# Eight row buffers, scatters by tile and later weight splits at the seam between attention and experts

## The chip, the cores and the metric

The kernel runs on one core of one Trainium2 chip. A time is the device time of one execution in microseconds (us). Besides that, one execution was profiled; its trace counts from the start of its own span. PE is the matrix engine (TensorE), DVE the vector engine, ACT the scalar engine, POOL is GpSimd, and SP issues most of the transfers.

## What is computed

Three stages follow each other. The output of attention, 1536 tokens of 512 numbers, is routed to two of eight experts for each token, and what comes back runs through a dense layer.

```python
# attention: 2 batches x 8 heads x 768 tokens, head size 64
k_sum = k.reshape(B, H, nb, 32, D).max(axis=3); v_sum = v.reshape(B, H, nb, 32, D).mean(axis=3)
scores_l = where(|i - j| < 16, scale * q @ k.T, -1e9)        # a window
scores_s = scale * q @ k_sum.T + log(32)                     # and 24 block summaries
a = softmax(concat(scores_l, scores_s)); attn = a @ concat(v, v_sum)
# routed experts: x is attn as 1536 x 512
noisy = x @ w_gate + log1p(exp(x @ w_noise)) * noise
top2, weights = two best of noisy, softmax over the two
out[n] = sum over its two experts e of weight * (relu(x[n] @ w1[e]) @ w2[e])     # 512 -> 1024 -> 512
# dense layer
h = out @ w_in; r = relu(h); y = (r * r) @ w_out                                  # 512 -> 2048 -> 512
```

## The kernel before

**Attention, with its own planner.** The attention stage is a list of nodes (`class Plan`), each with an engine, a cost, nodes that it depends on and buffers that it takes from a pool. The planner plays the list through in a model of the engines and emits the instructions in the order in which its model starts them, those with the longest chain of costs behind them first. So costs and edges decide the order, and each engine then runs its instructions in that order.

**Token rows.** The 1536 tokens are twelve tiles g = 0 to 11 of 128 rows. PE turns the attention output of a tile into rows in PSUM (L437), and DVE scales them into a buffer `xrow` (L441), one of six (pool `xr`). The gate works in four groups (`GROUPS`: tiles 0 to 5, 6 to 8, 9, and 10 with 11); it gives each row two places (k = 0 and 1) in the DRAM buffer `xg`, which is ordered by expert.

**Scatters.** POOL sends each tile's rows twice to `xg` with an indirect DMA (L461), 24 in all. Ahead of each goes a memset of a one-row tile `spacer` of 640 columns (L460), 1 column for tiles 6 to 8. A buffer of `xrow` is free when both scatters of its tile have landed. The order is tile 0 twice, then k = 0 of tiles 1 to 5, and then k = 1 of tiles 1 to 5, since the k = 0 nodes are chained and have the longer chain behind them.

**Expert 0's rows.** When the scatters of tiles 0 to 8 have landed, SP reads expert 0's part of `xg` back (`rows_load`, L522). The scatters of tiles 9 to 11 come after that. Those three tiles go to expert 0 on a shorter way too: DVE makes a one-hot matrix `pick` of each tile (L593), PE multiplies it into PSUM (`pull`, L510, from hi and lo parts `xpick` of the rows), and adds the rows read back (`rows_add`, L529). ACT (L249) and DVE (L254) split the sum into `xh` and `xl`.

**Weights.** Matrix products are done in three passes of fp32r, so each weight tile `wr` of 128x1024 is split into `wh` (ACT, L206) and `wl` (DVE, L210). The splits 0 and 1 belong to attention's planner and have a pool of their own; split 2 is the first that uses the pool `wsp1`, which is opened when attention's pools are closed and takes their memory.

**Units.** From there the order is written out in one loop: 64 units of the experts (8 for each), then 48 of the dense layer. Unit g does `h_unit` (12 matmuls of w1 with relu, hh on ACT L834, hl on DVE L835) and then `y_unit` of unit g - 1 (12 matmuls of w2, which need hh and hl). In the same loop stand the weight splits, and steps of other work at given units: `tables()` (routing tables on DVE, L929 to L1005, with a scatter of 24 zero rows to `xg`, L982), `fill(e)` (an indirect DMA of POOL that writes zero rows behind the rows of expert e, L920), `x_load(e)` (SP reads expert e's rows, L234), then DVE's transposes (L240).

**Blending.** Towards the end of the experts a token tile's two expert rows are gathered and blended (`mix`, L1210, stored to DRAM by L1215), read back with 32x32 blocks exchanged (`swap`, four transfers, L1219), and transposed by DVE (`flip`, L1230). The five numbers of `G0` say at which unit after its start each of these steps of a tile in 0 to 3 stands (gather, mix, swap, flip, and the split behind it). `y_store` (L858 to L866) writes an expert's output with eight transfers.

Of the kernel before, what the change touches and what calls it, by code (L numbers as in the profile page):

```python
# [19 lines left out]
QT = S // 128  # L20
# [3 lines left out]
E = 8  # L24
# [34 lines left out]
SPACE = 640  # L59
# [14 lines left out]
G0 = (0, 4, 5, 8, 9)  # L74
# [3 lines left out]
class Plan:  # L78
# [6 lines left out]
    def node(self, eng, cost, fn, *deps, take=(), wait=0.0, after=()):  # L85
        n = {"id": len(self.nodes), "eng": eng, "cost": cost, "fn": fn, "deps": deps, "after": after, "take": take,
             "wait": wait, "free": {}}
        self.nodes.append(n)
        return n
# [18 lines left out]
    def run(self):  # L108
        after = {n["id"]: [] for n in self.nodes}
        need = {}  # L110
        for n in self.nodes:
            before = {d["id"] for d in (*n["deps"], *n["after"])}
            need[n["id"]] = len(before)
            for d in before:
                after[d].append(n)
        then = {i: list(a) for i, a in after.items()}
# [33 lines left out]
def moe_pipeline_kernel(ctx: ExitStack, tc: tile.TileContext, qT, kT, vW, mk, idm, wg, noise, w1, w2, out):  # L150
# [105 lines left out]
    def attention(ctx):  # L256
# [4 lines left out]
        xr_p = ctx.enter_context(tc.tile_pool(name="xr", bufs=6))  # L261
# [17 lines left out]
        zt = ac.tile([128, CAP], F32, name="zt")  # L279
        ioc = ac.tile([128, CAP], F32, name="ioc")  # L280
        spacer = ac.tile([1, SPACE], F32, name="spacer")
# [4 lines left out]
        for b in range(B):  # L286
# [4 lines left out]
                     "gw": 1, "xr": 6, "k": LBUF, "w": LBUF, "q": LBUF},  # L291
# [167 lines left out]
        def scatter(g, k):  # L459
            nc.gpsimd.memset(spacer[:, 0:1] if 6 <= g < DIRECT else spacer, 0.0)  # L460
            i = nc.gpsimd.indirect_dma_start(out=xg, out_offset=bass.IndirectOffsetOnAxis(ap=slot_i[:, g, k:k + 1], axis=0),  # L461
                                             in_=xrow[g], in_offset=None)
            for j in scat:
                tc.declare_no_dep(i.ins, j.ins, reason="every slot is a row of its own")
            scat.append(i)
# [190 lines left out]
        for u in range(len(heads)):  # L656
# [38 lines left out]
            if u == 1:  # L695
                wvals_n = load(0.9, lambda: (nc.sync.dma_start(out=wg_sb, in_=wg), nc.sync.dma_start(out=nz, in_=noise)),
                               after=[last])
                zero_n = load(2.4, lambda: nc.sync.dma_start(
                    out=xg[0:CAP, :].rearrange("r d -> (r d)").rearrange("(p a c) -> p a c", p=128, a=4),
                    in_=zt[:, None, :].to_broadcast([128, 4, CAP])), set_n, after=[wvals_n])  # L700
# [41 lines left out]
        for g0, n in GROUPS:  # L742
# [11 lines left out]
            p_t["L", g0] = rt.tile([128, QT, 16], F32, name="L", bufs=len(GROUPS))[:, 0:n, :]  # L754
# [23 lines left out]
            for g in range(g0, g0 + n):  # L778
                for k in range(2):
                    sct[g, k] = node("G", 1.28 if 6 <= g < DIRECT else 1.77, lambda g=g, k=k: scatter(g, k), slot_n, xr_n[g], zero_n, *late,  # L780
                                     after=() if k or g >= DIRECT else list(sct.values())[-1:], wait=1.0)
# [12 lines left out]
        for i in range(W0):  # L794
            split = [node("A", 1.04, lambda i=i: w_hi(i), wl[i], after=[*split, slots_n[6]])]
            node("V", 1.22, lambda i=i: w_lo(i), *split)
# [121 lines left out]

    def fill(e):
        nc.gpsimd.indirect_dma_start(  # L920
            out=xg.rearrange("(g r) d -> g (r d)", r=4),
            out_offset=bass.IndirectOffsetOnAxis(ap=gi[0:XC // 4, e:e + 1], axis=0),
            in_=z4[0:XC // 4], in_offset=None)

    def tables():
# [45 lines left out]
        def by_expert(out, a):  # L971
# [4 lines left out]
        ri, gf = tbp.tile([128, 1], I32, name="tb_ri"), t("gf", E)  # L976
        tt(ri[0:n3], p[0:n3, 1, 0:1], rc[0:n3], OP.add)
        ts(gf, p[:, 0, 0:E], p4, OP.is_gt, NTOK / 4, OP.mult)
# [3 lines left out]
        nc.gpsimd.indirect_dma_start(out=xg, out_offset=bass.IndirectOffsetOnAxis(ap=ri[0:n3, 0:1], axis=0),  # L982
                                     in_=z4[0:n3, 0:DM], in_offset=None)
# [440 lines left out]
```

## Time and profile before

| what | value |
|---|---|
| runs | 678.84 us median of 3 (675.65, 678.84, 681.6) |
| the profiled execution | 677.83 us, of which its span is 675.8 us |
| mean granted clock of PE in it | 0.979 of full speed |
| PE busy | 637.6 us (94%) |
| DVE busy | 442.7 us (66%) |
| ACT busy | 366.2 us (54%) |
| POOL busy | 118.8 us (18%) |

In 40 slices of 16.9 us the page shows PE's busy tenths and its granted clock (tenths of full speed, 5 is 1.2 GHz and 9 about 2.4 GHz):

```profile
PE   5878776998999999999999999999999999999995
PEclk9989976999999999999999999999999999999998
```

The first seven slices, to 118 us, are attention and the seam to the experts. From the eighth on PE is busy nearly without a break. A time in what follows is a start in the trace; "[3.25 <-X]" behind an instruction is the idle time of its engine ahead of it and what ended it.

### The profile page before, as it was taken

What the parts mean: (1) busy time and instruction counts of PE and PEld (TensorE: products, weight loads), DVE (VectorE), ACT (ScalarE), POOL (GpSimd) and SP (SyncE); (2) the same over time, 40 slices, a digit from 0 to 9 for tenths busy, and PEclk for the clock granted to TensorE, in tenths of its full rate; (3) what the DMA queues carried; (4) which work ended last, traced back from release to release, by engine and by line L of the source; (5) the groups of instructions that cost most, each with busy time, mean ns of one, the idle gap of its engine ahead of it and who ended that gap; (6) DMA issues with size and microseconds to landing.
All of it is one profiled execution on the core that took longest, in us unless ns stands there. A gap on an engine that the chain in (4) does not pass through costs nothing. (4 is left out here: it accounts for less than half of the span.)

```text
span 675.8 us, 11334 instructions
## 1 busy us (share of the span) xinstructions
PE 637.6 (94%) x4062; PEld 572.0 (85%) x4062; DVE 442.7 (66%) x984; ACT 366.2 (54%) x708; POOL 118.8 (18%) x178
## 2 busy tenths in 40 slices
PE   5878776998999999999999999999999999999995
PEld 4766675898999999999999998888888888888884
DVE  4777856559687878677678867666555566544442
ACT  3846561456575667476667666654444454433431
POOL 4013385411001001700023001300043000300002
PEclk9989976999999999999999999999999999999998
DMA  8985135579999988788879888765356643333201
GB/s 215 233 206 180 49 157 214 196 218 327 367 280 326 290 293 252 237 234 273 265 245 389 249 280 244 271 157 161 119 160 196 186 144 110 141 108 96 92 1 66
DMA packets 72308, 138.96 MB, mean 206 GB/s; under 512 B 8873, under 2 KB 40313, under 8 KB 71462
## 3 DMA queue, kind: packets, MB, share of 16 engines
q1 hardware_dynamic: 66134, 115.92, 56.7%
q0 software_dynamic: 6112, 22.25, 8.7%
q8 instruction: 34, 0.56, 0.3%
q14 instruction: 28, 0.23, 0.1%
HBM read 103.27 MB, written 34.88 MB: 204 GB/s over the span
## 5 line engine op out<-in xcount | busy, mean ns | idle before, releaser
L813 PE MATMUL ph<-xl,wh 128*128 128x512 f32 (+8 forms) x448 | 162.4, 363 | 0.3 <-DVE xl L254 0.3
L811 PE MATMUL ph<-xh,wh 128*128 128x512 f32 (+8 forms) x448 | 162.7, 363 | 0.0
L812 PE MATMUL ph<-xh,wl 128*128 128x512 f32 (+8 forms) x448 | 162.3, 362 | 0.0
L210 DVE TENSOR_TENSOR wl<-wr,wh 128x1024 fp32r<-128x1024 f32 x112 | 136.7, 1221 | 37.9 <-ACT wh L206 35.3
L206 ACT ACTIVATE wh<-wr 128x1024 fp32r<-128x1024 f32 x112 | 117.5, 1049 | 13.1 <-DMA wr<-in_w_dram 8.0
L813 PEld LDWEIGHTS ph<-xl,wh 128*128 128x128 f32 x448 | 84.2, 188 | 8.3 <-DVE xl L254 0.7
L811 PEld LDWEIGHTS ph<-xh,wh 128*128 128x128 f32 x448 | 84.3, 188 | 7.6
L812 PEld LDWEIGHTS ph<-xh,wl 128*128 128x128 f32 x448 | 84.3, 188 | 7.6
L813 PE MATMUL acc<-hl,wh 128*128 128x416 f32 (+7 forms) x256 | 87.8, 343 | 1.6 <-DVE hl L835 1.6
L811 PE MATMUL acc<-hh,wh 128*128 128x416 f32 (+7 forms) x256 | 87.7, 343 | 0.8 <-ACT hh L834 0.8
L812 PE MATMUL acc<-hh,wl 128*128 128x416 f32 (+7 forms) x256 | 87.6, 342 | 0.0
L828 ACT ACTIVATE hr<-ph 128x512 f32<-128x512 f32 x48 | 28.7, 598 | 98.1 <-PE ph L813 95.8
L829 DVE SCALAR_TENSOR_TENSOR hg<-ph,hr 128x512 f32<-128x512 f32 x48 | 33.2, 692 | 66.9 <-ACT hr L828 64.4
L834 ACT ACTIVATE hh<-ph 128x416 fp32r<-128x416 f32 (+7 forms) x64 | 32.2, 503 | 80.5 <-PE ph L813 75.4
L812 PE MATMUL acc<-wh,hl 128*128 128x512 f32 x192 | 74.8, 390 | 0.0
L813 PE MATMUL acc<-wl,hh 128*128 128x512 f32 x192 | 74.7, 389 | 0.0
L811 PE MATMUL acc<-wh,hh 128*128 128x512 f32 x192 | 74.7, 389 | 0.0
L835 DVE SCALAR_TENSOR_TENSOR hl<-ph,hh 128x416 fp32r<-128x416 f32 (+7 forms) x64 | 36.5, 570 | 32.9 <-ACT hh L834 31.5
L832 DVE TENSOR_TENSOR hl<-hg,hh 128x512 fp32r<-128x512 f32 x48 | 33.3, 693 | 33.5 <-ACT hh L831 33.5
L831 ACT ACTIVATE hh<-hg 128x512 fp32r<-128x512 f32 x48 | 30.3, 632 | 38.0 <-DVE hg L829 37.2
L813 PEld LDWEIGHTS acc<-hl,wh 128*128 128x128 f32 x256 | 48.2, 188 | 2.3 <-DVE hl L835 2.2
L811 PEld LDWEIGHTS acc<-hh,wh 128*128 128x128 f32 x256 | 48.2, 188 | 1.2 <-ACT hh L834 1.1
(255 smaller groups left out, 921.4 us busy)
## 6 DMA issues: line engine op xcount, KB each, us to landing
wr<-in_w_dram SPq DMA_DIRECT2D x64, 512.0 KB
wr<-w2f SPq DMA_DIRECT2D x48, 512.0 KB
cr<-in_w_dram SPq DMA_DIRECT2D x32, 512.0 KB
w2f<-c SPq DMA_DIRECT2D x32, 256.0 KB
vB<-in_vW_dram SPq DMA_DIRECT2D x8, 576.0 KB
xin<-xg SPq DMA_DIRECT2D x16, 208.0 KB
kB<-in_kT_dram SPq DMA_DIRECT2D x16, 200.0 KB
yg<-ys SPq DMA_DIRECT2D x16, 192.0 KB
```

The lines of the kernel that those rows point to most:

```text
L206: nc.scalar.activation(out=hi_t[i], in_=raw_t[i], func=AF.Copy)
L210: nc.vector.tensor_tensor(out=lo_t[i], in0=raw_t.pop(i), in1=hi_t[i].bitcast(F32), op=OP.subtract)
L811: nc.tensor.matmul(out=o, lhsT=wh, rhs=xh, start=first, stop=False)
L812: nc.tensor.matmul(out=o, lhsT=wl, rhs=xh, start=False, stop=False)
L813: nc.tensor.matmul(out=o, lhsT=wh, rhs=xl, start=False, stop=last)
L828: nc.scalar.activation(out=r[:, 0:n], in_=p[:, 0:n], func=AF.Relu)
L829: nc.vector.scalar_tensor_tensor(out=gg[:, 0:n], in0=p[:, 0:n], scalar=0.0, in1=r[:, 0:n], op0=OP.max, op1=OP.mult)
L831: nc.scalar.activation(out=hh[:, 0:n], in_=gg[:, 0:n], func=AF.Copy)
L832: nc.vector.tensor_tensor(out=hl[:, 0:n], in0=gg[:, 0:n], in1=hh[:, 0:n].bitcast(F32), op=OP.subtract)
L834: nc.scalar.activation(out=hh[:, 0:n], in_=p[:, 0:n], func=AF.Relu)
L835: nc.vector.scalar_tensor_tensor(out=hl[:, 0:n], in0=p[:, 0:n], scalar=0.0, in1=hh[:, 0:n].bitcast(F32), op0=OP.max, op1=OP.subtract)
```

## The change

It has five parts.

1. `xr` has eight buffers in place of six. Room comes from the tile `L` of the gate, which now has as many columns as its group needs, and from `spacer`, which is gone: the memset ahead of a scatter now writes the first row of `zt`, a tile of zeros that attention holds anyway, 592 wide (before 416). The memset is 592 columns long where it was 640.
2. Scatter k = 1 of a tile stands right behind k = 0. The planner has a new kind of edge for it, `behind`, which orders but does not count in a node's rank.
3. The weight splits 0 and 1 stand behind the last `pick`, by the same kind of edge.
4. `fill(e)` no longer depends on the scatter of the 24 zero rows. That scatter's rows that would fall into the region of a fill are sent to rows of no use, for which six operations of 24x1 are added to `tables()` ahead of it. A memset of the 1x1 tile `gap` stands ahead of each fill.
5. In `G0` the third number is 6 in place of 5: `swap` of tiles 0 to 3 stands one unit later.

```diff
-SPACE = 640
+SPACE = 592
...
-G0 = (0, 4, 5, 8, 9)
+G0 = (0, 4, 6, 8, 9)
...
-        after = {n["id"]: [] for n in self.nodes}
+        after, then = ({n["id"]: [] for n in self.nodes} for _ in range(2))
         need = {}
         for n in self.nodes:
-            before = {d["id"] for d in (*n["deps"], *n["after"])}
+            ranked = {d["id"] for d in (*n["deps"], *n["after"])}
+            before = ranked | {d["id"] for d in n["behind"]}
             need[n["id"]] = len(before)
             for d in before:
                 after[d].append(n)
-        then = {i: list(a) for i, a in after.items()}
+            for d in ranked:
+                then[d].append(n)
...
-        xr_p = ctx.enter_context(tc.tile_pool(name="xr", bufs=6))
+        xr_p = ctx.enter_context(tc.tile_pool(name="xr", bufs=8))
...
-        zt = ac.tile([128, CAP], F32, name="zt")
+        zt = ac.tile([128, SPACE], F32, name="zt")
...
-        spacer = ac.tile([1, SPACE], F32, name="spacer")
...
-                     "gw": 1, "xr": 6, "k": LBUF, "w": LBUF, "q": LBUF},
+                     "gw": 1, "xr": 8, "k": LBUF, "w": LBUF, "q": LBUF},
...
         def scatter(g, k):
-            nc.gpsimd.memset(spacer[:, 0:1] if 6 <= g < DIRECT else spacer, 0.0)
+            nc.gpsimd.memset(zt[0:1, 0:1] if 6 <= g < DIRECT else zt[0:1], 0.0)
...
-            p_t["L", g0] = rt.tile([128, QT, 16], F32, name="L", bufs=len(GROUPS))[:, 0:n, :]
+            p_t["L", g0] = rt.tile([128, n, 16], F32, name=f"L{g0}", bufs=1)
...
-                                     after=() if k or g >= DIRECT else list(sct.values())[-1:], wait=1.0)
+                                     after=() if k or g >= DIRECT else list(sct.values())[-1:],
+                                     behind=[sct[g, 0]] if k else (), wait=1.0)
...
-            split = [node("A", 1.04, lambda i=i: w_hi(i), wl[i], after=[*split, slots_n[6]])]
+            split = [node("A", 1.04, lambda i=i: w_hi(i), wl[i], after=[*split, slots_n[6]], behind=[pick_n[NT - 1]])]
...
+    few = []
     def fill(e):
-        nc.gpsimd.indirect_dma_start(
+        nc.gpsimd.memset(gap, 0.0)
+        d = nc.gpsimd.indirect_dma_start(
...
+        for j in few:
+            tc.declare_no_dep(d.ins, j.ins, reason="rows of its own")
...
         tt(ri[0:n3], p[0:n3, 1, 0:1], rc[0:n3], OP.add)
+        ts(rem[0:n3], ri[0:n3], 3, OP.bitwise_and)
+        ts(aside[0:n3], pc[0:n3], float(XR), OP.mult, float(XR - 3), OP.add)
+        v.scalar_tensor_tensor(out=aside[0:n3], in0=rc[0:n3], scalar=float(1 - E * XR), in1=aside[0:n3], op0=OP.mult, op1=OP.add)
+        tt(far[0:n3], rem[0:n3], rc[0:n3], OP.is_gt)
+        tt(gf[0:n3, 0:1], ri[0:n3], aside[0:n3], OP.subtract)
+        ts(ri[0:n3], gf[0:n3, 0:1], far[0:n3], OP.mult, aside[0:n3], OP.add)
...
-        nc.gpsimd.indirect_dma_start(out=xg, out_offset=bass.IndirectOffsetOnAxis(ap=ri[0:n3, 0:1], axis=0),
-                                     in_=z4[0:n3, 0:DM], in_offset=None)
+        few.append(nc.gpsimd.indirect_dma_start(out=xg, out_offset=bass.IndirectOffsetOnAxis(ap=ri[0:n3, 0:1], axis=0),
+                                                in_=z4[0:n3, 0:DM], in_offset=None))
```

Three places show how the instructions of an engine move. The rows give the line, the operation, what it writes and reads, and the semaphores that it waits for. Line numbers after the change are one or two higher.

On DVE, at the rows of tiles 6 and 7, where attention's last heads end. `xrow<-pv,inv` is the scaling of a tile's rows; a wait for DMASW is one for the landing of indirect DMAs. Before:

```order
L441 TENSOR_TENSOR xrow<-pv,inv 128x512 [waits DMASW1_49,DMASW0_49,PE_49]
L425 COPY xh<-pv 128x128 [waits PE_49]
L425 COPY xl<-pv 128x128 [waits PE_49]
L441 TENSOR_TENSOR xrow<-pv,inv 128x512 [waits DMASW7_49,DMASW2_49]
L441 TENSOR_TENSOR xrow<-pv,inv 128x512 [waits DMASW3_49,DMASW0_49,PE_49]
L577 TENSOR_TENSOR sl<-pv,mall 128x48 [waits PE_49]
```

The same place after the change:

```order
L442 TENSOR_TENSOR xrow<-pv,inv 128x512 [waits PE_49] x2
L426 COPY xh<-pv 128x128 [waits PE_49]
L426 COPY xl<-pv 128x128 [waits PE_49]
L578 TENSOR_TENSOR sl<-pv,mall 128x48 [waits PE_49]
L582 TENSOR_REDUCE slot_i<-sl 128x6 [waits DVE_49]
L431 TENSOR_SCALAR inv<-sums 128x16 [waits Activation_49]
L432 RECIPROCAL inv<-inv 128x16 [waits DVE_49]
L442 TENSOR_TENSOR xrow<-pv,inv 128x512 [waits DMASW1_49,DMASW0_49,PE_49]
```

The scaling of tiles 6 and 7 waits for PE alone; the first that waits for landed scatters is that of tile 8, and it waits for the first two scatters. The order puts the gate's slots (L578, L582) ahead of it.

On ACT, from the last copies of attention to the second expert unit. `wh<-wr` is a weight split; the first two are splits 0 and 1, and the one with the long list of waits is split 2. Before:

```order
L206 ACTIVATE wh<-wr 128x1024 [waits DMAHW6_49]
L612 ACTIVATE an<-an 128x8 [waits DVE_49]
L206 ACTIVATE wh<-wr 128x1024 [waits DMAHW7_49]
L406 ACTIVATE et<-pt 120x512 [waits PE_49,Activation_49] x2
...
L249 ACTIVATE xh<-pt 128x416 [waits PE_49] x2
L206 ACTIVATE wh<-wr 128x1024 [waits DMAHW2_49,DMAHW3_49,DMAHW1_49,DMAHW4_49,DMAHW0_49,DMAHW5_49,DVE_49,Pool_49]
L834 ACTIVATE hh<-ph 128x416 [waits PE_49]
```

After the change:

```order
L456 ACTIVATE xpick_142<-xrow 128x512 [waits DVE_49]
L208 ACTIVATE wh<-wr 128x1024 [waits DMAHW6_49]
L208 ACTIVATE wh<-wr 128x1024 [waits DMAHW7_49]
L251 ACTIVATE xh<-ps 128x416 [waits PE_49] x2
L251 ACTIVATE xh<-pt 128x416 [waits PE_49] x2
L208 ACTIVATE wh<-wr 128x1024 [waits DMAHW2_49,DMAHW1_49,DMAHW3_49,DMAHW0_49,DMAHW4_49,DVE_49,DMAHW5_49,Activation_49,Pool_49]
L836 ACTIVATE hh<-ph 128x416 [waits PE_49]
```

Splits 0 and 1 have moved from among attention's last copies to behind the last `xpick`; their halves on DVE (`wl`) have moved in the same way behind the last `pick`. Split 2 waits for POOL in both kernels. The count of POOL that it waits for is, in both, that of the memset ahead of the 24th scatter, since the tile lies in memory that attention gave back.

On SP, around the last `y_store` of the experts. `x<-x2d` is a swap (four transfers), `x2d<-x` the store of a blended tile, `yg<-ys` the y_store, `wr` a weight tile. Before:

```order
L1219 DMA x_4697<-x2d_2003 32x4x128 [waits DMAHW7_49]
L1215 DMA x2d_2004<-x_4754 128x512 [waits DMAHW0_49,DVE_49]
L903 DMA w2f<-c_4608 128x512 [waits DMAHW1_49]
L200 ISA
L200 DMA wr<-in_w_dram 128x1024 [waits DVE_49]
L1219 DMA x_4754<-x2d_2004 32x4x128 [waits DMAHW3_49,DMAHW0_49]
...
L875 DMA cr<-in_w_dram 128x1024 [waits DMAHW7_49]
L863 DMA yg<-ys 32x11x128 [waits DVE_49]
```

After the change:

```order
L877 DMA cr<-in_w_dram 128x1024 [waits DMAHW3_49]
L865 DMA yg<-ys 32x11x128 [waits DMAHW4_49,DVE_49]
...
L868 DMA yg<-ys 30x128 [waits DMAHW3_49]
L202 ISA
L202 DMA wr<-in_w_dram 128x1024 [waits DMAHW4_49,DVE_49]
L1235 DMA x_4765<-x2d_2003 32x4x128 [waits DMAHW5_49]
L1235 DMA x_4765<-x2d_2003 32x4x128 [waits DMAHW6_49]
L1235 DMA x_4765<-x2d_2003 32x4x128 [waits DMAHW7_49]
```

The swap of the second tile (x2d_2004 before, x2d_2003 after) stood ahead of the eight transfers of `y_store` and now stands behind them and behind one weight tile; its first transfer no longer waits for a store that was issued two places ahead of it.

## Rows read from the trace of the kernel before

**Rows 1.** windows: PE PEld DVE ACT POOL busy us (instructions), PEclk, DMA share, GB/s

```profile
100.00:120.00 20.00, 14.02 (x116) 12.18 (x113) 11.80 (x46) 3.29 (x8) 11.73 (x17) 0.67 0.57 207
120.00:140.00 20.00, 20.00 (x212) 18.21 (x211) 13.75 (x40) 10.54 (x17) 6.79 (x7) 0.97 0.58 213
140.00:160.00 20.00, 18.61 (x99) 18.17 (x98) 13.08 (x31) 12.88 (x21) 1.86 (x2) 1.00 0.89 287
```

**Rows 2.** waits of PE, 126-200 us: total us, times, longest

```profile
PE acc L813 <- DVE hl L835: 1.4, 1, 1.4
PE ph L813 <- DVE xl L254: 0.3, 1, 0.3
```

**Rows 3.** waits of PE, 200 us to the end

```profile
PE acc L811 <- ACT hh L834: 0.8, 1, 0.8
PE acc L813 <- DVE hl L835: 0.2, 1, 0.2
```

**Rows 4.** waits of all engines, 76 to 100 us

```profile
DVE xrow L441 <- DMA xg<-xrow,slot_i: 3.9, 1, 3.9
...
PE pv L437 <- DVE xrow L441: 3.2, 1, 3.2
```

**Rows 5.** timeline of POOL: start, us, instruction, [idle ahead <- releaser]

```profile
77.84 1.17 POOL L461 DMA_INDIRECT xg<-xrow,slot_i  x1 [10.05 <-issue]
...
79.85 0.97 POOL L461 DMA_INDIRECT xg<-xrow,slot_i  x1 [0.17 <-issue]
80.82 0.62 POOL L460 MEMSET spacer<- 1x640 f32 x1
...
114.55 0.97 POOL L461 DMA_INDIRECT xg<-xrow,slot_i  x1 [6.88 <-DVE sf L585]
...
122.66 0.62 POOL L460 MEMSET spacer<- 1x640 f32 x1
...
126.36 1.82 POOL L940 MEMSET z<- 128x2048 f32 x1 [1.94 <-DMA xg<-xrow,slot_i]
...
140.11 0.93 POOL L920 DMA_INDIRECT xg<-z,tb_gi  x1 [3.84 <-DVE tb_pre L996]
```

**Rows 6.** timeline of ACT, weight split 2

```profile
125.68 1.05 ACT L206 ACTIVATE wh<-wr 128x1024 fp32r<-128x1024 f32 x1
```

**Rows 7.** timeline of DVE, first expert units

```profile
126.76 1.23 DVE L210 TENSOR_TENSOR wl<-wr,wh 128x1024 fp32r<-128x1024 f32 x1 [0.36 <-ACT wh L206]
128.25 0.59 DVE L835 SCALAR_TENSOR_TENSOR hl<-ph,hh 128x416 fp32r<-128x416 f32 x1 [0.26 <-ACT hh L834]
```

**Rows 8.** timeline of PE, first matmul of the experts, third of the first y_unit

```profile
125.13 0.46 PE L811 MATMUL ph<-xh,wh 128*128 128x416 f32 x1
...
130.13 0.35 PE L813 MATMUL acc<-hl,wh 128*128 128x416 f32 x1
```

**Rows 9.** timeline of DVE: place of the few zero rows; expert 1's rows arrive

```profile
134.36 0.14 DVE L932 TENSOR_TENSOR tb_ri<-px,rc 24x1 int32<-24x1 f32 x1
...
152.60 1.17 DVE L240 STREAM_TRANSPOSE xtt<-xin 128x448 f32<-128x448 f32 x2 [5.94 <-DMA xin<-xg]
```

**Rows 10.** waits of all engines, 380 to 405 us

```profile
ACT wh L206 <- DMA wr<-w2f: 5.1, 1, 5.1
```

**Rows 11.** timeline of SP: expert 1's rows; the weight tile behind the y_store

```profile
145.58 1.95 SPq L234 DMA_DIRECT2D xin<-xg  x4
...
383.44 0.36 SPq L200 DMA_DIRECT2D wr<-in_w_dram  x1
```

**Rows 12.** window around a stretch of PE at half clock

```profile
94.00:100.70 6.70, 6.70 (x54) 6.30 (x56) 4.20 (x14) 1.64 (x3) 5.92 (x9) 0.50 0.43 172
```

**Rows 13.** timeline of DVE, the second flip and the hl behind it

```profile
384.64 0.70 DVE L1230 STREAM_TRANSPOSE z<-x 128x512 f32<-128x512 f32 x1
...
386.30 0.54 DVE L835 SCALAR_TENSOR_TENSOR hl<-ph,hh 128x374 fp32r<-128x374 f32 x1
```

**Rows 14.** timeline of PE, the matmul that needs that hl

```profile
389.70 0.33 PE L813 MATMUL acc<-hl,wh 128*128 128x374 f32 x1
```

More of the change, by code (lines that the diff above doesn't have):

```diff
@@ L83, in __init__, with node @@
         self.nodes, self.room, self.clock = [], {p: (c, []) for p, c in room.items()}, clock
-    def node(self, eng, cost, fn, *deps, take=(), wait=0.0, after=()):
+    def node(self, eng, cost, fn, *deps, take=(), wait=0.0, after=(), behind=()):
         n = {"id": len(self.nodes), "eng": eng, "cost": cost, "fn": fn, "deps": deps, "after": after, "take": take,
-             "wait": wait, "free": {}}
+             "wait": wait, "free": {}, "behind": behind}
         self.nodes.append(n)
@@ L699, in attention @@
                     out=xg[0:CAP, :].rearrange("r d -> (r d)").rearrange("(p a c) -> p a c", p=128, a=4),
-                    in_=zt[:, None, :].to_broadcast([128, 4, CAP])), set_n, after=[wvals_n])
+                    in_=zt[:, None, 0:CAP].to_broadcast([128, 4, CAP])), set_n, after=[wvals_n])
             plan.uk = k0
@@ L976, in tables @@
         ri, gf = tbp.tile([128, 1], I32, name="tb_ri"), t("gf", E)
+        rem, aside, far = tbp.tile([128, 1], I32, name="tb_rem"), t("aside", 1), t("far", 1)
         tt(ri[0:n3], p[0:n3, 1, 0:1], rc[0:n3], OP.add)
+        ts(rem[0:n3], ri[0:n3], 3, OP.bitwise_and)
[4 more added lines that the diff above has]
+        ts(ri[0:n3], gf[0:n3, 0:1], far[0:n3], OP.mult, aside[0:n3], OP.add)
         ts(gf, p[:, 0, 0:E], p4, OP.is_gt, NTOK / 4, OP.mult)
```

## The prediction

> **What bounds the kernel now.** I read the windows first. From 120 us on PE works without a gap (20.00 of 20.00 us) at nearly full clock, while between 100 and 120 us it is busy for 14.02 us at 0.67 of its clock [rows 1]. Then I read PE's waits. Behind 126 us PE is idle for 1.4 and 0.3 us [rows 2], and for 0.8 and 0.2 us [rows 3], and for nothing else until the last unit. So PE bounds the kernel from the first expert unit on, and there are two ways only to gain: let the expert units begin earlier, or take away these 2.7 us.
>
> What sets their begin is read backwards. Ahead of 100 us DVE stands for 3.9 us with tile 6's rows, because all six buffers wait for scatters that have not landed, and PE stands 3.2 us behind it [rows 4]. POOL meanwhile sends a scatter every 1.76 us (0.17 between, 0.97 for the issue and 0.62 for the memset [rows 5]), which no buffer speeds up.
>
> **Term 1, the units begin earlier.** With eight buffers the rows of tiles 6 and 7 wait for nothing, and tile 8 waits for the first two scatters (the order shows this); those were issued at 77.84 and 79.85 [rows 5], far ahead. So the 3.9 us go. The two `wl` of 1.23 us each [rows 7] also leave the middle of gate 9's chain on DVE, up to 2.5 us more; they lie behind the last `pick`, where DVE has nothing to do until the rows come back. By DVE's chain the first expert matmul, at 125.13 before [rows 8], could then come at 125.13 - 3.9 - 2.5 = 118.7 (121.2 with the stall alone).
>
> But POOL's chain is not moved with it, and it now decides. Weight split 2 lies in memory that attention gave back; it waits for the last memset, the one ahead of the 24th scatter. That memset begins at 122.66 and ends at 123.28 [rows 5]; the split began at 125.68 [rows 6], so before there were 2.4 us to spare. What shortens POOL's chain is the width: 48 columns of 640 are at most 0.62 x 48 / 640 = 0.047 us, and as part of a memset is fixed I take 0.04. Sixteen of these memsets lie on the chain (eleven between the first twelve scatters, then five between the late six, which start when expert 0's rows have been read back, 114.55 before): 0.64 us. The last memset ends at 122.64, and from there: split 2 on ACT at 122.74; `wl` on DVE 1.08 us later (125.68 to 126.76 [rows 6, 7]); 1.23 us for it; then `hl` of unit 0, which stands behind it on DVE, 0.59 us [rows 7]. PE can use it at 122.74 + 1.08 + 1.23 + 0.59 = 125.64. The matmul that does is the third of the first y_unit, and it came at 130.13 [rows 8]. So term 1 is 130.13 - 125.64 = -4.5. For this the first expert matmul must come by 125.64 - 5.0 = 120.6, as PE takes 130.13 - 125.13 = 5.0 us to get there. The 118.7 keep this, the 121.2 miss it by 0.6. Bounds: -3.9 if the splits' move gives nothing or the memsets don't shrink; -6.4 if split 2 doesn't wait for the memset after all.
>
> What is late next? The routing tables' first operation on DVE and their first matmul wait until the last scatter has landed. POOL's memset of `z` waited for that too and began at 126.36 [rows 5], so this lands at about 125.7 now. On DVE the operation stands behind `hl` of unit 0 and another `wl`, at 125.6 + 1.23 = 126.9; 1.2 us cover it. If that cover is gone, each us later is one us of PE.
>
> **Term 2, fill(1).** Expert 1's rows come late: DVE waits for them 5.94 us until 152.60 [rows 9], and PE's 1.4 and 0.3 us [rows 2] are the `hl` and the `xl` queued behind that wait. Ahead of the read stands fill(1), which began at 140.11 after 3.84 us of idle time on POOL [rows 5], that is, the few-rows scatter's issue was over at 136.27 and its landing was waited for. Without this wait fill(1) could start at 136.3, plus the six operations put ahead of the scatter. The nearest row, 24x1, is 0.14 us [rows 9]; each needs the one before it, so I take 0.22, 1.3 us in all, and 0.4 for the memset and the gaps: 138.0, 2.1 us earlier against the units around it. That is more than 1.7, so both stalls go: -1.7. Bounds 0 (something else holds the read, SP's queue for one) and -1.7. The six operations themselves are hidden on DVE, which is busy for 13.75 of 20 us there [rows 1].
>
> **Term 3, the swap.** SP now meets each swap's wait for a stored tile one unit later, when it is over. The weight tile queued behind it came late enough that ACT stood 5.1 us for it [rows 10], and PE's 0.8 and 0.2 us [rows 3] are the price. These go: -0.9 of the 1.0. The opposite risk is that the second swap stands behind the y_store and the weight tile that went out at 383.44 [rows 11]; that is rival C.
>
> The kind of edge `behind`, the tile `L` and the `gap` memset cost nothing on a path: they are planner's work, memory, and one short operation on POOL, which is idle there.
>
> **Sum.** 677.83 - 4.5 - 1.7 - 0.9 = 670.7 against the profiled execution. The median of the runs is 1.0 above that one, so 671.7.
>
> **Rival B, the clock.** In the new kernel PE ends its first two h_units before `hh` and `hl` of unit 0 are there: from 118.7 on they take 4.6 us, to 123.3; `hh` stands behind split 2 on ACT, so it comes at about 124.3, and `hl` at 125.6. This is 1 us and, after two matmuls, another 0.9; if the matmuls begin a us sooner, it is 2.9 in all. Before, a stall of 3.2 us [rows 4] was followed by 6.7 us of full work at a granted clock of 0.50, the 1.2 GHz level [rows 12], and a stall of 1.4 us [rows 2] by none (1.00 from 140 to 160 us [rows 1]). The new gap lies between the two. The Trainium skill, "TensorE: Matmul & The Clock Gate", section "What's actually happening", says that "the default state is throttled, and activity releases the throttle", so it speaks for a loss whenever PE has stood; the trace agrees for 3.2 us and not for 1.4. If the clock falls, 6.7 us at half of it cost 3.4 us, and half such a stretch 1.7: 671.7 + 1.7 to 3.4 = 673.4 to 675.1.
>
> **Rival C, the second flip.** The swap's four issues end about 1.95 us (as the four of expert 1's rows [rows 11]) behind 383.44 + 0.36, at 385.8. The flip began at 384.64 before, and `hl` at 386.30 stands behind it on DVE, done at 386.84 [rows 13]; PE used it at 389.70 [rows 14], so 2.9 us are spare. Expert 1's rows came 152.60 - 147.53 = 5.1 us after their last issue. If the swap takes as long, the flip begins at 390.9, 6.2 us late, and PE loses 3.3; if it takes 1.8 or less, nothing. In the middle term 3 turns from -0.9 into +1.5: 674.1.
>
> **Rival D, the change does not do what it says.** Tile 6's rows are no longer late, but the pulls' start hangs on PE's last attention work, at half clock, and the units begin when they did. Then only terms 2 and 3 are left: 677.83 - 2.6 + 1.0 = 676.2. Against it: PE's 3.2 us of idle time are put down to that very `xrow` [rows 4].
>
> **Rival F, better.** Split 2's wait doesn't bind, by -6.4: 669.8.
>
> **Rival E, slower.** Two scatters in a row now read the same buffer, and POOL may take longer for such a pair. The only such pair of the first twelve is the first one, 77.84 to 79.85, 2.01 us instead of 1.76 [rows 5], though its first issue (1.17) is the first of all. If every scatter took 0.25 us more, the chain would end 24 x 0.25 = 6 us later: term 1 would be +1.5, the time 677.7. It decides at 0.30 us more, the level of before, and for over 1% slower each scatter would need some 0.58 us more. The late six were sent in pairs before too, and kept to 1.78 (the first at 114.55, the memset behind the fifth at 122.66, 0.97 for its issue [rows 5]: 7.14 over four), so I give it little.
>
> **Chances.** Forecast 0.42, B 0.25, C 0.13, F 0.09, D 0.06, E 0.05. A measurement of this kernel can tell about 1% from no change, that is 6.8 us, so faster means under 672.1. The forecast lies so near this line that I count three quarters of it as faster; with F that is 0.41. Same: a quarter of the forecast, B, C and D, 0.54. Slower: E, 0.05. The range goes from 668.0 (F, and 1.8 for the spread of runs) to 676.5 (D and just over). The forecast's own range is 670.5 to 672.5.
>
> **What would show it.** Right: no wait of DVE's `xrow` for a landing; POOL's scatters at 1.7 us; the last memset ending at about 122.6 with ACT's split 2 right behind it; PE's third matmul of the first y_unit at about 125.6; no wait of PE for `hl` near 150 us and none near 400 us. Wrong: a granted clock of 0.50 behind 125 us (B), a wait of DVE's flip for `x<-x2d` (C), the first expert matmul behind 121 us (D), a pitch above 1.8 us (E), split 2 ahead of the last memset (F). The sum also falls if attention itself takes another time than before, for I take its first 88 us as unchanged.

## The result, and the profile after

On the chip where both were timed the changed kernel takes 672.87 us (median of 11 runs, 671.07 to 680.65) and the kernel before 681.60 (11 runs, 675.65 to 687.09). The ratio is 0.989, with an interval from 0.987 to 0.992: 1.1% faster. The profiled execution takes 672.87 us, and its span is 670.7 us, 5.1 less than the 675.8 before. The prediction said 671.7 (668.0 to 676.5).

PE decides the time, and its matmuls of the units are the same 2688 in both kernels. So the start of one and the same matmul in two traces tells where the 5.1 us came from. The third matmul of the first y_unit is number 27; the others are counted in the same way.

| PE's stretch | before | after | difference | forecast |
|---|---|---|---|---|
| start of matmul 1, the first of the experts | 125.13 | 120.52 | -4.6 | -6.4 to -3.9 |
| start of matmul 27, the first that needs `hl` | 130.13 | 127.02 | -3.1 | -4.5 (term 1) |
| 27 to 49, the first y_unit | 4.57 | 4.65 | +0.1 | 0 (rival B: +1.7 to +3.4) |
| 49 to 201, expert 1's rows arrive in it | 30.85 | 30.26 | -0.6 | -1.7 (term 2) |
| 201 to 1481 | 230.59 | 230.60 | 0.0 | 0 |
| 1481 to 1531, the swaps | 10.32 | 9.25 | -1.1 | -0.9 (term 3) |
| 1531 to the end | 269.33 | 268.97 | -0.4 | 0 |

The windows of the new trace (columns as in [rows 1]):

```profile
88.00:94.00 6.00, 5.94 (x81) 5.17 (x78) 4.74 (x25) 5.77 (x28) 5.33 (x8) 1.00 0.47 176
100.00:114.00 14.00, 11.00 (x49) 10.29 (x49) 9.60 (x32) 3.37 (x6) 6.96 (x12) 0.65 0.59 203
120.00:140.00 20.00, 18.91 (x110) 17.62 (x105) 15.09 (x47) 11.13 (x17) 8.56 (x12) 1.00 0.75 266
140.00:160.00 20.00, 18.77 (x99) 18.02 (x98) 14.60 (x36) 12.58 (x20) 1.02 (x2) 1.00 0.87 278
```

At 88 to 94 us, where PE stood for 3.2 us before [rows 4], it is busy for 5.94 of 6.00. But from 120 to 140 us it is no longer busy throughout: 18.91 of 20. POOL's timeline says what it waits for there, with ACT's and PE's behind it:

```profile
79.48 1.17 POOL L462 DMA_INDIRECT xg<-xrow,slot_i  x1 [12.53 <-DVE bi L388]
...
81.44 0.97 POOL L462 DMA_INDIRECT xg<-xrow,slot_i  x1 [0.17 <-issue]
...
115.69 0.96 POOL L462 DMA_INDIRECT xg<-xrow,slot_i  x1 [7.61 <-DMA xtt<-xg]
...
123.53 0.58 POOL L461 MEMSET zt<- 1x592 f32 x1
...
133.93 0.90 POOL L998 DMA_INDIRECT xg<-z,tb_ri  x1 [4.97 <-DVE tb_gf L996]
...
135.13 0.94 POOL L927 DMA_INDIRECT xg<-z,tb_gi  x1 [0.22 <-DVE tb_size L947]
```

```profile
124.14 1.06 ACT L208 ACTIVATE wh<-wr 128x1024 fp32r<-128x1024 f32 x1 [2.41 <-POOL zt L461]
```

```profile
120.52 0.46 PE L813 MATMUL ph<-xh,wh 128*128 128x416 f32 x1
...
125.75 0.43 PE L813 MATMUL acc<-hh,wh 128*128 128x416 f32 x1 [0.44 <-ACT hh L836]
...
127.02 0.46 PE L815 MATMUL acc<-hl,wh 128*128 128x416 f32 x1 [0.65 <-DVE hl L837]
```

The last memset ends at 123.53 + 0.58 = 124.11, and split 2 starts at 124.14, after 2.41 us in which ACT waited for that memset by name. PE's two small waits, 0.44 and 0.65 us, are those for `hh` and `hl` of unit 0. In the kernel before, split 2 came 2.4 us after the memset [rows 5, 6] and PE had no wait there. The waits of PE behind that:

```profile
PE acc L815 <- DVE hl L837: 1.6, 2, 0.9
...
PE ph L815 <- DVE xl L256: 0.3, 1, 0.3
```

Of the 1.6 us for `hl` 0.65 belong to unit 0, and 0.9 to the unit that stands behind expert 1's rows, where it was 1.4 [rows 2]; the 0.3 for `xl` is still there. From 200 us on PE has no wait left over 0.15 us in this profile, where it had 0.8 and 0.2 [rows 3]. A later profile of this kernel (the third in the table below) has one of 0.9 us for `hl` at 223.6 us, so the row "201 to 1481" is not 0.0 in every pair.

### The profile page after: what moved, and what is told of

Read it like the earlier page. It is cut to its first block, busy times and chain, and to the rows that moved or that the text cites. A ratio compares the mean times of both kernels' runs of the same rounds, so it can differ in the third digit from the quotient of the medians.

```text
span 670.7 us, 11350 instructions
## 1 busy us (share of the span) xinstructions
PE 638.4 (95%) x4062; PEld 571.7 (85%) x4062; DVE 443.4 (66%) x990; ACT 366.2 (55%) x708; POOL 117.8 (18%) x185
## 5 line engine op out<-in xcount | busy, mean ns | idle before, releaser
L395 ACT ACTIVATE es<-z,bi 128x120 f32<-128x120 f32 x96 | 36.7, 384 | 23.2 <-DVE bi L388 23.1
```

Of the source, the lines that this page charges most:

```text
L395: nc.scalar.activation(out=e_t[s][:, i, h], in_=z, func=AF.Exp, bias=bi, scale=-1.0, accum_out=sums[:, b * QT + t0 + i, c:c + 1])
```

## The experiments

Two theories stand against each other on the main point. **POOL's chain**: with the change, PE's matmul 27 is held by the last memset, through split 2, `wl` and `hl`. **The chain of rows**: it is held by xrow, gate, pulls and the rows read back, and split 2's wait is only beside it. Smaller questions: what frees the rows that stood for 3.9 us in the kernel before, the buffers or the order; where the first scatter's time comes from; what terms 2 and 3 are worth. Edits are given against the changed kernel. Time points of all profiles are in one table behind the runs.

**The changed kernel again**, unaltered, for what varies from one execution to the next.

> The changed kernel once more, unaltered. In its first profile PE ran at half clock from 70.0 to 76.8 us, behind a stall of 1.6 us that stood in the kernel before too and brought no half clock there, though PE, DVE, ACT and POOL had the same instructions in the same order up to that place. Theory 'chance': the spell comes and goes from execution to execution; without it the first scatter starts near 77.1 instead of 79.5, the last memset ends near 122, the third matmul of the first y_unit comes near 125.5 instead of 127.0 and the span is 669 to 669.5. Theory 'the change moved it': the spell stands at 70 us again, first scatter 79.3 to 79.6, third matmul 126.8 to 127.2, span 670.5 to 671.

It took 675.19 us (10 runs) beside 678.91 for the kernel before on that chip, ratio 0.994 (0.991 to 0.997). The spell of half clock at 70 us was gone, but others came earlier, and the first scatter was at 80.42. In the first pair of profiles, the changed kernel first and the kernel before second:

```profile
70.00:76.80 6.80, 6.36 (x56) 4.12 (x57) 3.24 (x18) 2.47 (x9) 0.00 (x0) 0.50 0.01 4
```

```profile
70.00:76.80 6.80, 6.17 (x105) 4.40 (x102) 5.07 (x31) 3.71 (x13) 0.00 (x0) 1.00 0.01 4
```

A stall of 1.6 us stands ahead of one and the same matmul, near 70 us, in all fourteen profiles. Behind it the same stretch of time has PE at 0.50 in one execution and at 1.00 in the other: 56 matmuls in 6.36 us of work against 105 in 6.17. Two later profiles turn it round. The kernel before then has the spell (0.50 from 70.3 to 77.1 us) and its first scatter at 79.69; the changed kernel's third profile has no spell there and its first scatter at 77.60. So "chance" holds, though not the number: the first scatter came anywhere from 77.6 to 81.6 us in fourteen profiles, while ahead of it the two kernels differ in nothing but the widths of two memsets on POOL.

**Six buffers.**

```diff
-        xr_p = ctx.enter_context(tc.tile_pool(name="xr", bufs=8))
+        xr_p = ctx.enter_context(tc.tile_pool(name="xr", bufs=6))
...
-                     "gw": 1, "xr": 8, "k": LBUF, "w": LBUF, "q": LBUF},
+                     "gw": 1, "xr": 6, "k": LBUF, "w": LBUF, "q": LBUF},
```

> The changed kernel with six row buffers again; scatters stay in the order of tiles. Theory 'order frees them': sent by tile, both scatters of tiles 0 and 1 are out by about 85 us and landed some 3 us later, so the rows of tiles 6 and 7, due at 89.7, hardly wait with six buffers either; no wait of xrow above 0.5 us, first expert matmul and span within 0.7 us of the changed kernel. Theory 'the buffers free them': the wait of 3 to 4 us for a landing comes back at tile 6 or 7, the first expert matmul is 3 to 4 us later (about 124) and the time 1 to 3 us longer.

675.31 us, against 675.19 for the changed kernel on the same chip. No xrow waits for a landing; the rows of tiles 6 and 7 come at 88.83 and 89.43. In the kernel before, these two scalings, the seventh and the eighth, stand so:

```profile
88.20 0.69 DVE L441 TENSOR_TENSOR xrow<-pv,inv 128x512 f32<-128x512 f32 x1
...
93.16 0.69 DVE L441 TENSOR_TENSOR xrow<-pv,inv 128x512 f32<-128x512 f32 x1 [3.88 <-DMA xg<-xrow,slot_i]
```

So the rows that stood were tile 7's and not, as the prediction read it, tile 6's. Tile 6 takes the buffer of tile 0, whose scatters go first; tile 7 takes that of tile 1, whose second scatter was the eighth in the old order, issued at 90.39. This is why the order by tiles alone is enough.

**The old order of scatters.**

```diff
-                                     behind=[sct[g, 0]] if k else (), wait=1.0)
+                                     wait=1.0)
```

> The changed kernel with the old order of scatters (k = 0 of tiles 1 to 5 ahead of k = 1), eight buffers. Theory 'the buffers free them': tiles 6 and 7 need no freed buffer, tile 8 needs tile 0's, which goes first in either order; no wait of xrow above 0.5 us, time within 0.7 us of the changed kernel. Theory 'order frees them': a wait of 2 to 4 us for a landing, at tile 8 or 9, and the time 1 to 3 us longer.

677.27 us; its ratio to the kernel before is 0.997 (0.993 to 1.000) and overlaps that of the changed kernel (0.991 to 0.997), so the 2 us are not told apart from nothing. No xrow waits for a landing here either (tiles 6 and 7 at 91.75 and 92.35, with a first scatter at 81.50). Each of the two parts frees the rows by itself; together they bring no more.

**Splits 0 and 1 free again.**

```diff
-            split = [node("A", 1.04, lambda i=i: w_hi(i), wl[i], after=[*split, slots_n[6]], behind=[pick_n[NT - 1]])]
+            split = [node("A", 1.04, lambda i=i: w_hi(i), wl[i], after=[*split, slots_n[6]])]
```

> The changed kernel with weight splits 0 and 1 free to be planned where they were. Theory 'POOL's chain binds': the first expert matmul comes up to 2.5 us later (120.5 to 123), but the third matmul of the first y_unit, held by the last memset, moves by at most 1 us if the first expert matmul is behind 122, else not at all; time 0 to +0.7. Theory 'the chain of rows binds': the third matmul moves as much as the first one, +2 to +2.5, and the time with it.

675.00 us, no more than the changed kernel's 675.19. The first expert matmul comes 41.6 us behind the first scatter, 0.5 to 2.7 later than in the changed kernel's three profiles, and matmul 27 comes 2.90 us behind the last memset as there. POOL's chain binds, and the splits' move gains nothing that the time shows while it does.

**The fills wait for the 24 zero rows again.**

```diff
-        nc.gpsimd.memset(gap, 0.0)
-        d = nc.gpsimd.indirect_dma_start(
+        nc.gpsimd.indirect_dma_start(
...
-        for j in few:
-            tc.declare_no_dep(d.ins, j.ins, reason="rows of its own")
...
-        ts(rem[0:n3], ri[0:n3], 3, OP.bitwise_and)
-        ts(aside[0:n3], pc[0:n3], float(XR), OP.mult, float(XR - 3), OP.add)
-        v.scalar_tensor_tensor(out=aside[0:n3], in0=rc[0:n3], scalar=float(1 - E * XR), in1=aside[0:n3], op0=OP.mult, op1=OP.add)
-        tt(far[0:n3], rem[0:n3], rc[0:n3], OP.is_gt)
-        tt(gf[0:n3, 0:1], ri[0:n3], aside[0:n3], OP.subtract)
-        ts(ri[0:n3], gf[0:n3, 0:1], far[0:n3], OP.mult, aside[0:n3], OP.add)
```

> The changed kernel with the dependency of the fills on the scatter of the 24 zero rows restored, and without the six operations and the memset ahead of a fill. Theory 'the landing was the price': fill(1) starts 3 to 4 us behind the scatter's issue instead of 0.3, relative to the third matmul of the first y_unit some 2 us later than in the changed kernel; PE's stalls for hl and xl of expert 1 near 150 to 160 us sum to 2.0 to 3.5 us instead of the 0 to 1.2 of the changed kernel's profiles; time +1 to +2.5. Theory 'the read itself is late': the stalls grow by less than 0.5 us; time within 0.5.

676.36 us beside 680.62 before, ratio 0.998 (0.994 to 1.002). The fill starts 3.73 us after the scatter's issue again. PE's stalls are 0.9 and 0.3 us, less than expected; in the changed kernel's second profile, which had the same half clock in the first y_unit, there are none. Matmuls 49 to 201 take 30.23 us here and 28.84 there. The second profile is the fastest of its kind, though: three more kernels with the early fill and the same fall of the clock (six buffers, old order, swaps back) take 29.45 to 29.51. So the landing had a price of 0.7 to 1.4 us, near or under the low end of the +1 to +2.5 that was expected of it. The changed kernel was not run on this chip; its ratios elsewhere (0.989 to 0.994) have intervals that overlap this one. The read itself changes too. SP and DVE in this kernel, and then in the changed kernel's second profile:

```profile
137.91 0.36 SPq L202 DMA_DIRECT2D wr<-in_w_dram  x1
144.95 1.96 SPq L236 DMA_DIRECT2D xin<-xg  x4
...
151.89 1.17 DVE L242 STREAM_TRANSPOSE xtt<-xin 128x448 f32<-128x448 f32 x2 [5.40 <-DMA xin<-xg]
```

```profile
139.20 0.36 SPq L202 DMA_DIRECT2D wr<-in_w_dram  x1
142.82 1.95 SPq L236 DMA_DIRECT2D xin<-xg  x4
...
150.88 1.17 DVE L242 STREAM_TRANSPOSE xtt<-xin 128x448 f32<-128x448 f32 x2 [3.92 <-DMA xin<-xg]
```

The read is issued 7.04 us behind a weight tile with the wait, and 3.62 us behind it without. Its rows are there 6.94 us after its first issue in the one and 8.06 us in the other. Early, it follows closer on that weight tile.

**The swaps at the old unit.**

```diff
-G0 = (0, 4, 6, 8, 9)
+G0 = (0, 4, 5, 8, 9)
```

> The changed kernel with the swaps at the old unit. Theory 'SP's wait was the price': ACT waits 3 us or more for a weight tile near 395 us again, PE stalls 0.8 to 1.0 us for hh and hl there, and the small stall for hl near 395 (0.14 to 0.83 us in the changed kernel's profiles, behind the second flip) goes; net time +0.2 to +0.9. Theory 'swaps don't matter': no stall of either kind above 0.2 us, time within 0.2.

675.83 us beside the same 680.62, ratio 0.994 (0.990 to 0.999). Its waits from 380 to 405 us:

```profile
ACT wh L208 <- DMA wr<-w2f: 5.1, 1, 5.1
...
PE acc L813 <- ACT hh L836: 0.8, 1, 0.8
...
PE acc L815 <- DVE hl L837: 0.2, 1, 0.2
```

These are the waits of the kernel before [rows 3, 10], to the tenth. Matmuls 1481 to 1531 take 10.31 us, 1.06 more than the changed kernel's 9.25. Over all profiles it is 10.31 to 10.79 with the old swap (three) and 8.95 to 9.96 with the later one (eleven). SP's wait was the price.

**Short memsets ahead of the late six.**

```diff
-            nc.gpsimd.memset(zt[0:1, 0:1] if 6 <= g < DIRECT else zt[0:1], 0.0)
+            nc.gpsimd.memset(zt[0:1, 0:1] if 6 <= g else zt[0:1], 0.0)
```

> The changed kernel with 1x1 memsets ahead of the last six scatters too (as ahead of those of tiles 6 to 8). Theory 'POOL's chain binds': the last memset ends 2.4 to 2.9 us earlier against the first scatter (42.0 to 42.3 behind it instead of 44.6 to 44.9), weight split 2 starts right then or when ACT is free, the gap of PE ahead of the first y_unit shrinks to under 0.8 us, so no half clock follows it, and the third matmul comes at the first expert matmul + 5.0 to 5.5; time 1.5 to 3.5 shorter than the changed kernel. Theory 'the chain of rows binds': time within 0.5. Rival 'the spacing is needed': indirect DMAs closer together land later, and the tables' first operation on DVE waits for them; nothing gained.

671.52 us beside the same 680.62, ratio 0.989 (0.985 to 0.994); the two kernels of the same batch that have the long memsets took 676.36 and 675.83.

```profile
120.61 0.09 POOL L461 MEMSET zt<- 1x1 f32 x1
```

```profile
120.73 1.06 ACT L208 ACTIVATE wh<-wr 128x1024 fp32r<-128x1024 f32 x1 [3.09 <-POOL zt L461]
```

```profile
122.34 0.43 PE L813 MATMUL acc<-hh,wh 128*128 128x416 f32 x1 [0.57 <-ACT hh L836]
...
123.61 0.45 PE L815 MATMUL acc<-hl,wh 128*128 128x416 f32 x1 [0.65 <-DVE hl L837]
```

The last memset ends 42.5 us behind the first scatter instead of 44.3 to 44.9. Split 2 starts 0.03 us behind it, and matmul 27 comes 2.91 us behind it, as in the changed kernel. What moves POOL's chain moves PE.

**All wide memsets half as wide**, on two chips.

```diff
-            nc.gpsimd.memset(zt[0:1, 0:1] if 6 <= g < DIRECT else zt[0:1], 0.0)
+            nc.gpsimd.memset(zt[0:1, 0:1] if 6 <= g < DIRECT else zt[0:1, 0:SPACE // 2], 0.0)
```

> The changed kernel with all wide memsets half as wide (296 columns). Theory 'POOL's chain binds': pitch 1.43 instead of 1.72 us, the last memset ends 4.5 to 4.8 us earlier against the first scatter (about 40.2 behind it), expert 0's rows are read back 3 us earlier too, and the third matmul comes at the first expert matmul + 5.0; time 1.5 to 4 shorter than the changed kernel. Rival 'the spacing is needed': POOL's issue of an indirect DMA grows above 0.97 us or the landing above 2.7 us behind it, and nothing is gained.

> The changed kernel with memsets half as wide, again, for a comparison on one chip with the changed kernel: 4 to 9 us shorter than it, third matmul at the end of the last memset + 2.9 (or the first expert matmul + 5.0, where that is later).

On the chip of the last three runs it took 666.78 us (4 runs, 666.05 to 667.27), ratio 0.983 (0.975 to 0.991), the shortest time seen, with the last memset 39.5 us behind the first scatter and matmul 27 another 2.91 behind that. On another chip it took 684.89 us (4 runs, 683.97 to 685.43), ratio 1.011 (1.005 to 1.017), where the changed kernel took 674.40; the expectation of 4 to 9 us shorter failed. The same 16 us of both traces, the fast one first:

```profile
84.00:100.00 16.00, 13.52 (x211) 11.83 (x207) 13.69 (x77) 10.34 (x44) 14.03 (x24) 1.00 0.49 184
```

```profile
84.00:100.00 16.00, 9.36 (x96) 7.40 (x92) 6.45 (x46) 5.34 (x25) 12.52 (x20) 0.79 0.47 177
```

PE, DVE and ACT are busy for 47 to 69% as long in the slow one, at about the same DMA rate and with POOL's scatters at the same 1.47 us. The waits of PE and ACT there:

```profile
PE ps L377 <- DVE bi L388: 4.8, 2, 2.6
...
PE pt L403 <- issue: 0.8, 2, 0.4
```

```profile
ACT es L395 <- DVE bi L388: 3.6, 1, 3.6
ACT es L395 <- issue: 2.9, 1, 2.9
ACT et L407 <- remote: 2.5, 2, 2.1
```

They wait for each other, and where the wait has another cause the profile has no name for it ("issue", "remote"). No xrow waits for a landing. Why the engines stand there on one chip and not on the other stays open; on each of the two it is four runs and one profile.

**All memsets 1x1.**

```diff
-            nc.gpsimd.memset(zt[0:1, 0:1] if 6 <= g < DIRECT else zt[0:1], 0.0)
+            nc.gpsimd.memset(zt[0:1, 0:1], 0.0)
```

> The changed kernel with 1x1 memsets ahead of all scatters. In seven profiles of kernels with the change the third matmul of the first y_unit came 2.90 to 2.91 us behind the end of the last memset. Theory 'POOL's chain binds until the rows do': a scatter every 1.27 us, the last memset ends 36 to 36.5 us behind the first scatter (39.5 with half as wide memsets), and split 2 no longer waits for it, but stands behind ACT's four xh copies; the third matmul comes at the first expert matmul + 5.0 to 5.3, no longer at the memset + 2.9; time 0.3 to 1.5 shorter than with half as wide memsets. Rival 'the spacing is needed': scatters this close land late (more than 3 us behind their issue) or POOL's issue grows; time equal or longer than with half as wide memsets.

687.63 us (4 runs), ratio 1.016 (1.010 to 1.022), on the chip where half as wide memsets were slow. The rows of tile 6 come at 100.75 us (100.24 with half as wide memsets on this chip) instead of 88 to 92, and the first expert matmul at 135.42. Matmul 27 comes 4.97 us behind that and 10 us behind the last memset: here the chain of rows binds. As a faster kernel it is a miss; that the spacing is needed on this chip is what both short versions show, since they differ from the changed kernel in the memsets alone. It was not tried on the other chip.

**Both kernels again, on that same chip.**

> The changed kernel, unaltered, for a comparison on one chip. Third matmul at the end of the last memset + 2.9. If PE stands 2.7 us or more ahead of the first y_unit, half clock begins within 3 us behind it; if less than 1 us, none.

> The kernel before, unaltered, a second profile. Theory 'chain of rows binds before': the third matmul of the first y_unit comes at the first expert matmul + 5.0 and 4 us or more behind the end of the last memset; where the first scatter starts later (half clock in attention) the wait of xrow for a landing is longer and all else follows.

The changed kernel took 674.40 us, ratio 0.993 (0.990 to 0.997), and the kernel before 680.62. The two rows of the second profile of the kernel before that stand against [rows 4] and [rows 8]:

```profile
DVE xrow L441 <- DMA xg<-xrow,slot_i: 3.9, 1, 3.9
```

```profile
131.58 0.35 PE L813 MATMUL acc<-hl,wh 128*128 128x416 f32 x1
```

The stall for the landing is 3.9 us again. Matmul 1 stands at 126.58 and matmul 27 exactly 5.00 us behind it and 5.99 us behind the last memset (125.59): in the kernel before, the chain of rows binds.

All profiles in one table. "Memset" is the end of the last memset, "gap" PE's idle time ahead of the first y_unit, "27 to 49" the time of the first y_unit from its third matmul on.

| kernel | first scatter | memset | matmul 1 | matmul 27 | 27 behind memset | gap | 27 to 49 | span |
|---|---|---|---|---|---|---|---|---|
| before | 77.84 | 123.28 | 125.13 | 130.13 | 6.85 | 0 | 4.57 | 675.8 |
| before again | 79.69 | 125.59 | 126.58 | 131.58 | 5.99 | 0 | 4.54 | 678.7 |
| changed | 79.48 | 124.11 | 120.52 | 127.02 | 2.91 | 0.44 | 4.65 | 670.7 |
| changed, second | 80.42 | 125.33 | 119.32 | 128.23 | 2.90 | 2.86 | 6.76 | 673.1 |
| changed, third | 77.60 | 121.89 | 117.81 | 124.79 | 2.90 | 0.71 | 4.68 | 670.7 |
| six buffers | 78.58 | 122.69 | 116.75 | 125.59 | 2.90 | 2.79 | 6.12 | 670.5 |
| old order | 81.50 | 126.87 | 120.84 | 129.77 | 2.90 | 2.88 | 7.00 | 675.9 |
| splits free | 81.58 | 126.46 | 123.13 | 129.36 | 2.90 | 0.18 | 4.66 | 673.1 |
| fills wait | 80.09 | 125.06 | 119.05 | 127.96 | 2.90 | 2.86 | 6.65 | 674.1 |
| swaps back | 79.98 | 124.79 | 118.90 | 127.69 | 2.90 | 2.74 | 6.11 | 674.1 |
| late six short | 78.22 | 120.70 | 116.99 | 123.61 | 2.91 | 0.57 | 4.64 | 668.2 |
| half as wide | 80.06 | 119.59 | 116.96 | 122.50 | 2.91 | 0 | 4.65 | 665.1 |
| half as wide, second chip | 80.61 | 130.33 | 134.19 | 139.19 | 8.86 | 0 | 4.57 | 682.8 |
| all 1x1 | 77.79 | 130.34 | 135.42 | 140.39 | 10.05 | 0 | 4.55 | 684.7 |

## Why the prediction was right, point by point

**The mechanism of term 1 was right.** The prediction had split 2 held by the memset ahead of the 24th scatter, and with it `wl`, `hl` and the third matmul of the first y_unit, 2.90 us later by its sum (1.08 + 1.23 + 0.59). In all ten profiles where PE reached the first y_unit before that, the distance is 2.90 or 2.91 us, while matmul 1 moves between 116.75 and 123.13. Shortening only the late memsets moved matmul 27 with them.

**Its size was off in the profiled pair: -3.1 instead of -4.5.** The step that failed is the first one, "I take its first 88 us as unchanged". The instructions were the same in the same order, but the profiled execution had a spell of half clock at 70 us that that of the kernel before hadn't, and the first scatter went out at 79.48 instead of 77.84 (in the other pair it is the other way round, see above). Against the first scatter, the sum is right: matmul 27 came 52.3 and 51.9 us behind it in the two profiles of the kernel before, and 47.5, 47.8 and 47.2 in the three of the changed one, 4.6 us less in the mean. A smaller part of the same term went the other way: the chain from the first scatter to the last memset shrank by 45.44 - 44.63 = 0.8 us in the first pair, against the 0.64 of the sum, although the rows were read back later (the late six began at 115.69, 9.1 us behind the 18th scatter; 114.55 and 8.5 before).

**Of its parts, the order and the buffers do one thing between them, and the splits' move does nothing yet.** The prediction gave the 3.9 us to the eight buffers; six with the new order do as well, and eight with the old order too. It also took the rows for tile 6's where they were tile 7's, which changes nothing in the sum. The up to 2.5 us of the splits show in the chain of rows (0.5 to 2.7 us, one profile against three), but PE cannot use them behind POOL's chain, as the sum had it.

**Rival B was right where its condition was met.** It gave the fall of the clock behind a gap between 1.4 and 3.2 us. In the table, the five profiles with a gap of 2.7 to 2.9 us take 6.1 to 7.0 us for the first y_unit, the others, with 0 to 0.7, take 4.5 to 4.7. The second profile of the changed kernel, with the granted clock (0.50) in the third column from the end, and PE there:

```profile
126.30:133.00 6.70, 5.80 (x17) 4.71 (x18) 5.61 (x13) 2.82 (x5) 1.97 (x2) 0.50 0.70 236
```

```profile
126.97 0.68 PE L813 MATMUL acc<-hh,wh 128*128 128x416 f32 x1 [2.86 <-ACT hh L836]
...
128.23 0.71 PE L815 MATMUL acc<-hl,wh 128*128 128x416 f32 x1 [0.23 <-DVE hl L837]
```

The price in the first y_unit is 1.5 to 2.4 us, at the low end of the forecast's 1.7 to 3.4 and just under it. With the fall and the early fill, matmuls 27 to 201 take 35.6 to 36.5 us, no less than the 35.4 and 35.7 of the kernel before; without the fall they take 33.6 to 34.9. So where the clock falls, what term 2 gains is lost again. One of three profiles of the changed kernel had it, too few to test the chance of 0.25. The Trainium skill, "TensorE: Matmul & The Clock Gate", section "What's actually happening", says that PE's default is the lower clock. The falls behind 2.7 to 2.9 us agree with it; the stalls of up to 0.7 us cost no clock. There is a bitter side: where the chain of rows runs faster than POOL's, PE comes to the first y_unit earlier only to stand longer, and its clock fell in all five such profiles.

**Term 2 was mis-sized: -0.6 to -1.1 instead of -1.7.** Matmuls 49 to 201 take 30.26 and 30.11 us in the first and third profile of the changed kernel, 30.85 and 31.16 in the two of the kernel before; the second profile of the changed kernel (28.84) had lost its time to the clock just ahead. The fill does start 2.1 us earlier against the units, as forecast (3.5 us behind matmul 49 instead of 5.4 and 5.8). The step that failed is that the rows would come as much earlier. The read takes 7.9 to 8.2 us in the profiles of the changed kernel and 6.9 to 7.0 in those with the wait; it is now issued closer behind a weight tile. That this tile is the cause was not tried by itself, and one profile speaks against it: with half as wide memsets, on the chip where that was fast, the early read took 7.0 us just as close behind its weight tile (3.5 us). In the other kernels with the early fill it took 7.6 to 9.2. So the cause stays open. The bound from 0 to -1.7 held.

**Term 3 was right: -1.1 instead of -0.9**, and the experiment gives 1.06 back. Rival C came in small: DVE waited for the swapped tiles,

```profile
DVE z L1246 <- DMA x<-x2d: 4.8, 2, 2.9
```

2.9 us in the longest case, and PE lost 0.15 us by it in this trace and up to 0.8 in others (a wait for `hl` near 395 us, which the kernel with the old swap doesn't have). The prediction took the two together as a choice; both happened. Its price for C was added up wrongly: the middle between 0 and a loss of 3.3 us is 1.65, which turns term 3 into +0.75 and the time into 673.4, not +1.5 and 674.1.

**Rivals D, E and F did not come.** Against the first scatter, matmul 1 came 41.0 us behind it where it had been 47.3 (D). The pitch of the scatters behind the first pair was 1.72 us, with two in a row from one buffer (E). Split 2 started behind the last memset (F).

**The total.** The sum gave -7.1 for the profiled pair; -5.1 came, of which 1.4 are missing in term 1, 1.1 in term 2, and 0.6 came back in term 3 and at the end. By medians the gain was 8.7, 3.7 and 5.1 us on three chips (681.60, 678.91 and 679.53 before, 672.87, 675.19 and 674.40 after). So 671.7 for 672.87 is right within what one execution tells, but that the two lie so close is in part luck. The base, 678.84, was the median of three runs, and eleven runs gave 681.60, 2.8 more; on that chip the gain by medians, 8.7, was 1.6 more than the sum's 7.1, while it was 2.0 less in the profiled pair. And the forecast's edge of 1% is where the measured ratios lie: 0.989, 0.994 and 0.993.

## What to carry to other kernels

A freed tile hands its last user's lateness to whoever takes the memory next: when a stage is made to start earlier, look for the last instruction of the old stage on each engine, however small (here a memset that only spaces DMAs), and for what takes its memory. A distance that stays the same to 0.01 us over many variants, while everything around it moves, is a sign of what binds; a variant that moves the suspect alone is the test. And an earlier start that only lets PE stand at the next wait can lose time: in the five profiles with 2.7 to 2.9 us there, the clock fell and the unit behind it took 1.5 to 2.4 us more.

## What the runs showed of the hardware

PE's half clock comes at other places from one execution to the next though the instructions are the same: at 70 us behind a stall of 1.6 us in one profile and not in another. With such spells at different places the first scatter stood anywhere between 77.6 and 81.6 us. A difference of 2 us between two profiles says nothing of a change as long as such spells lie ahead of it; counted from the first scatter, matmul 27 of one and the same kernel agrees within 0.4 us (two profiles before) and 0.6 us (three after).

A stall costs more than its idle time in the trace. Two matmuls of a chain start 0.19 us apart but last 0.35, so the 1.39 us of idle time ahead of the matmul at 154.70 in the kernel before is a start 1.73 us behind the last, 1.54 us lost.

Indirect DMAs in a long row can come too close together, so that engines stand. Twelve of them 1.72 us apart did no such harm on any chip here, nor did twelve 1.47 apart on one chip; on another PE, DVE and ACT stood for 2 to 4 us at a time, in part with no cause that the profile names, and the kernel was 18 us longer. It is not the distance alone: the scatters of tiles 6 to 8 follow each other at about 1.27 us in the changed kernel too. A memset of one row on POOL has a fixed part: 0.09 us for 1 column, 0.33 for 296 and 0.58 for 592.
